# Weights of a fused attention and feed-forward kernel converted step by step, its mixing, gate and outputs regrouped

## The chip, the cores and the metric

The kernel runs as one program on one core of a Trainium2 chip. The metric is the device time of one execution in microseconds (us); the number quoted for a kernel is the median of its timed executions. A core has a matrix engine (PE in the profile, its weight loads shown apart as PEld), a vector engine (DVE), a scalar engine (ACT), GpSimd (POOL) and a queue engine (SP) that issues most of the transfers. DVE, ACT and POOL each work through their instructions in the order in which they were written; an instruction that waits holds up those behind it. Matrix products land in PSUM, which has eight banks.

## What is computed

Three stages follow each other, for a batch of 2 with 768 positions. The sizes are 8 heads of 64, a model width of 512, a mixing rank of 32, and feed-forward widths of 2048 and 1024. The inputs are float64.

```
mask   = argmax(q_n . c_n) == argmax(k_n . c_n)        # clustered attention, per head
x      = softmax(where(mask, q k^T / 8, -1e9)) v       # (2, 768, 512)

u      = x + ((x^T @ U) @ V)^T                         # mixing over the positions
x      = u + relu(u @ w_ch1) @ w_ch2                   # first feed-forward

h      = relu(x @ w_in)                                # second feed-forward, gated
conv   = conv_w[0]*h[s-1] + conv_w[1]*h[s] + conv_w[2]*h[s+1]
out    = (h * sigmoid(conv)) @ w_out
```

## The kernel before

**Three stages.** Attention runs over 96 steps (`step(n)`, 6 tiles for each of 16 heads). Then come the first feed-forward in 8 chunks of 256 columns and the second in 4. To keep float32 accuracy on the faster product format, every operand is split in a rounded high part and a low rest (`parts`: a cast on one engine, a subtraction on another), and each product is made of three: high by high, high by low, low by high.

**Code order is engine order.** Nothing is rescheduled. Work beside the products is placed by hand: generators yield after each group of matrix products, and `side(columns)` then issues one piece of waiting work: one entry of `aside`, one entry of `mixing`, and, for each 4096 columns of product, one `pump` of the weight conversion.

**Weights.** A chunk's weights come as float64 in jobs of 512 columns: two jobs for a wide matrix (`queue_wide`), two for a tall one (`queue_tall`). A job is a transfer (SP), a scaling (`job_base`, ACT), three integer operations on DVE (`job_word`: low, high, sign) that make a float32 word, and the put: a cast to the high part on ACT and a subtraction for the low part on POOL. The put of a wide matrix in the first feed-forward also forms four sums on POOL, and its last two casts on ACT (`rest`, L532) read those sums.

**First feed-forward.** `ff_h(c, b)` makes chunk c for batch element b by seven block products (Strassen's scheme) of 6 matrix products each, in four PSUM banks (`ps_a`); DVE combines them, ACT applies relu and casts (L822, L823) and POOL subtracts (L824). `ff_a(c, b)` makes eight groups `acc` of 6 products of 384 columns in three shared banks (`ps_t`, where mixing also lands); after each, DVE adds the bank to the sum `xa` (L845).

**Mixing** of one batch element is one entry `mt` (48 small products and the split of its result `tt`: per quarter a cast on ACT, a subtraction on DVE and a second cast on ACT), six entries `mu` (a product and a DVE addition of 128x512 onto x, L616), and six entries `mx` (four transposes and a copy on ACT). For the second batch element this stands after attention, between the groups of the first `ff_a(0, 0)` and `ff_h(1, 0)`; then `form_last` forms the operands of that element.

**Second feed-forward.** `g_h(c, b)` makes four groups `g` of 12 products; ACT applies relu into `h`. `gate(c, b)` makes, for two halves of 128x768 in SBUF, the convolution (one ACT instruction, two on DVE, L890 and L891), the sigmoid on ACT (L894), the product on POOL (L895), a cast on ACT and a subtraction on DVE (L900). `g_o(c, b)` makes six groups `po` of 6 products of 512 columns, each added to the output by DVE (L917, a copy on ACT for the first chunk).

## Time and profile before

| what | value |
|---|---|
| median of 3 executions | 715.45 us (715.01 to 715.98) |
| the profiled execution | 715.09 us, its span 713.3 us |
| busy share of the span | PE 92%, PEld 78%, DVE 71%, ACT 52%, POOL 41% |
| chain of work that ended last | PE 60%, DVE 22%, waiting to issue 7%, ACT 5%, POOL 5% |
| mean granted clock of PE | 0.98 of full speed |

The profile is one execution. A row of a stretch gives each engine's busy time and number of instructions, the clock that PE was granted (1.00 is full speed) and the load of the transfers. A row of time gives start, duration, engine, line, operation and tiles of an instruction, and in square brackets how long its engine had been idle before it and what it waited for. A row of waits gives who waited for whom: the sum in us, how often, and the longest. Ends of products on PE are modelled and overlap, so its pace is read from one start to another.

### The profile page before, as it was taken

To read this page: it belongs to the slowest core of one execution; us is meant where nothing else is said; L and a number is where in the kernel's file an instruction comes from. 1 tells how busy PE (TensorE), PEld (TensorE's weight loads), DVE (VectorE), ACT (ScalarE), POOL (GpSimd) and SP (SyncE) were. 2 spreads that over 40 slices of the span, in tenths; PEclk is the share of its full clock that TensorE was granted. 3 is DMA by queue.
4 is the path that set the end of the run, shared out by engine and by line. 5 is a ranking of instruction groups with operands and counts; after the bars stand their busy time and mean duration, and the time that the engine had idled before them with its cause. 6 is when DMAs were issued, how large, how long until landed. Compare 5 with 4: busy or idle time off the path is not lost.

```text
span 713.3 us, 10476 instructions
## 1 busy us (share of the span) xinstructions
PE 654.3 (92%) x3846; PEld 553.7 (78%) x3846; DVE 508.1 (71%) x890; ACT 371.9 (52%) x719; POOL 295.7 (41%) x299
## 2 busy tenths in 40 slices
PE   8999999999999987887799999999999698978896
PEld 5766767666767656887799999999989697966784
DVE  6887787878787656574657667584686768697665
ACT  6767667667676633443434344444443564653431
POOL 4645334535434624334635353636413432352221
PEclk9999999999999999999899999999999899999999
DMA  7687458354551011010212022130112110130003
GB/s 184 127 174 166 97 122 204 75 129 83 136 149 30 1 60 59 1 60 0 89 59 89 32 90 75 44 110 9 60 59 84 36 59 4 59 116 1 0 30 148
DMA packets 17860, 55.50 MB, mean 78 GB/s; under 512 B 3120, under 2 KB 3760, under 8 KB 17808
## 3 DMA queue, kind: packets, MB, share of 16 engines
q1 hardware_dynamic: 14208, 40.08, 18.5%
q0 software_dynamic: 3600, 14.75, 10.5%
q8 instruction: 30, 0.49, 0.3%
q14 instruction: 22, 0.18, 0.1%
HBM read 50.19 MB, written 3.15 MB: 75 GB/s over the span
## 4 chain that ended last, share of the span: by engine, by line
PE 60%; DVE 22%; issue 7%; ACT 5%; POOL 5%; DMA 0%; DVEq 0%; POOLq 0%
PE pv L399 8%; PE tr L383 7%; PE acc L841 4%; PE sc L345 4%; PE acc L842 3%; PE pb L781 3%; PE acc L843 3%; PE pd L781 3%; PE sc L356 3%; DVE cv L891 3%; PE pa L781 3%; PE g L876 3%; PE g L875 3%; PE g L874 3%; DVE e L362 3%
## 5 line engine op out<-in xcount | busy, mean ns | idle before, releaser
L841 PE MATMUL acc<-r,vh 128*128 128x384 f32 x256 | 90.1, 352 | 17.0 <-DVE xa L845 13.2
L362 DVE TENSOR_SCALAR_CACHE_REDUCE e<-sc 128x768 f32<-128x768 f32 x96 | 91.5, 954 | 12.2 <-PE sc L356 11.3
L374 ACT ACTIVATE e<-sc,nb 128x768 f32<-128x768 f32 x96 | 87.0, 906 | 9.5 <-DVE e L362 8.9
L842 PE MATMUL acc<-r,vh 128*128 128x384 f32 x256 | 88.0, 344 | 1.8 <-POOL r L824 1.8
L845 DVE TENSOR_TENSOR xa<-acc,xa 128x384 f32<-128x384 f32 x128 | 68.1, 552 | 29.4 <-PE acc L843 29.2
L843 PE MATMUL acc<-r,vl 128*128 128x384 f32 x256 | 87.8, 343 | 0.0
L383 PEld LDWEIGHTS tr<-identf,e 128*128 128x128 f32 x576 | 64.9, 140 | 25.7 <-issue 5.6
L383 PE MATMUL tr<-identf,e 128*128 128x128 f32 x576 | 81.2, 276 | 1.4 <-ACT tt L605 0.7
L399 PE MATMUL pv<-pt,rv 128*64 128x384 f32 x384 | 72.9, 498 | 0.0
L390 DVE COPY pt<-tr 128x384 f32<-128x384 f32 x96 | 53.0, 552 | 22.3 <-PE tr L383 21.4
L390 ACT COPY pt<-tr 128x384 f32<-128x384 f32 x96 | 46.1, 480 | 41.9 <-PE tr L383 41.8
L841 PEld LDWEIGHTS acc<-r,vh 128*128 128x128 f32 x256 | 49.6, 194 | 23.1 <-DVE xa L845 18.3
L547 POOL TENSOR_TENSOR vl<-wx,vh 128x512 fp32r<-128x512 f32 x24 | 32.9, 1371 | 72.0 <-ACT vh L546 67.6
L345 PE MATMUL sc<-ab 128*128 128x384 f32 x192 | 57.2, 380 | 2.0 <-ACT e L374 1.4
L895 POOL TENSOR_TENSOR h<-h,cv 128x768 f32<-128x768 f32 x16 | 32.1, 2007 | 53.0 <-ACT cv L894 51.8
L842 PEld LDWEIGHTS acc<-r,vh 128*128 128x128 f32 x256 | 49.8, 195 | 2.5 <-POOL r L824 2.3
L824 POOL TENSOR_TENSOR r<-q,r 128x384 fp32r<-128x384 f32 x16 | 16.2, 1014 | 81.1 <-ACT r L823 68.0
L843 PEld LDWEIGHTS acc<-r,vl 128*128 128x128 f32 x256 | 49.7, 194 | 0.0
L356 PE MATMUL sc<-cd 80*128 80x384 f32 x192 | 49.6, 340 | 0.0
L459 DVE SCALAR_TENSOR_TENSOR wy<-wb,wy 128x512 int32<-128x512 int32 (+1 forms) x44 | 30.1, 685 | 23.0 <-ACT wb L450 19.1
L399 PEld LDWEIGHTS pv<-pt,rv 128*64 128x64 f32 x384 | 24.3, 136 | 26.7 <-issue 24.4
L450 ACT ACTIVATE wb<-raw 128x512 f32<-128x512 f32 (+3 forms) x52 | 33.8, 649 | 10.3 <-DVE wx L463 6.7
(246 smaller groups left out, 1612.2 us busy)
## 6 DMA issues: line engine op xcount, KB each, us to landing
raw<-in_w_dram SPq DMA_DIRECT2D x32, 512.0 KB, 3.8
...
```

The lines of the kernel that those rows point to most:

```text
L345: nc.tensor.matmul(ps[:, f, 0:HS], ab[:, 0, c0:c0 + P], ab[:, 1, f * HS:(f + 1) * HS], start=True, stop=False)
L356: nc.tensor.matmul(ps[:, f, 0:HS], cd[0:80, 0, c0:c0 + P], cd[0:80, 1, f * HS:(f + 1) * HS], start=False, stop=True)
L362: nc.vector.tensor_scalar(out=e, in0=ps[:, :, 0:HS], scalar1=-SCALE, scalar2=3e38, op0=ALU.mult, op1=ALU.min, accum_out=nb,)
L374: nc.scalar.activation(e, ps[:, :, 0:HS], AF.Exp, scale=SCALE, bias=nb, accum_out=st["sum", n // NT][:, n % NT:n % NT + 1])
L383: nc.tensor.transpose(pt[:, k, :], e[:, i, k * P:(k + 1) * P], identf)
L390: (nc.scalar.copy if i == 0 else nc.vector.tensor_copy)(to, st.pop(("t", n, i)))
L399: nc.tensor.matmul(acc[i * D:(i + 1) * D], vts[b, h // 2][:, h % 2, k], pt[:, k, i * NK:(i + 1) * NK].rearrange("p a b -> p (a b)"), start ...
L781: nc.tensor.matmul(o, l[:, k, w], r[:, k], start=first and not more, stop=last, skip_group_check=more)
L841: nc.tensor.matmul(acc, wh[:, f, ds_], r[:, 0], start=f == 0, stop=False)
L842: nc.tensor.matmul(acc, wh[:, f, ds_], r[:, 1], start=False, stop=False)
L843: nc.tensor.matmul(acc, wl[:, f, ds_], r[:, 0], start=False, stop=f == 1)
L845: nc.vector.tensor_add(o, acc, o)
```

## The change

**Conversion.** `pump` with its plan for the feed-forward is replaced by `tick`. One tick issues at most one step of a put (`puts`) and at most one word step (`words`): the scaling, the first DVE operation, nothing, the second, the third. The put of a wide matrix is seven steps. Up to three finished words wait until the tile that they go to has been read for the last time (`opens`). Ticks come once for every 4, then 6, then 12 times 384 columns.

**Mixing.** The result is accumulated in PSUM: an entry `mx` is now three transposes of x and one product with `tt` into the same bank, followed by one copy on ACT; the six entries `mu` with their DVE additions are gone, and eight entries `mx` replace twelve. The second copy of `tt` is made by POOL. For the second batch element `mt` stands ahead of the first group of `ff_a(0, 0)`, and the last two groups of `ff_a(0, 0)` stand behind `ff_h(1, 0)`.

**Gate.** It works on quarters of 128x384 whose sums lie in the four banks of `ps_a`; the product moves from POOL to DVE, the last subtraction from DVE to POOL. It is issued in ten parts, three to four per group of products. The groups `g` land in `ps_t`.

**Outputs.** `g_o` takes two chunks at once: 12 products per group, one addition or copy where there were two. The order of the groups changes with it. The subtractions in `form_after` move from DVE to POOL.

The diff, cut:

```diff
+    def tick():
+        clock[0] += 1
+        for j in fly:
+            words.extend([lambda f=THIN[k], j=j: f(j) for k in sorted(THIN) if k > j["at"]])
+        fly.clear()
+        if puts and puts[0][0] in opened:
+            puts.pop(0)[1]()
+        if words:
+            words.pop(0)()
+        elif begun and clock[0] - begun[0]["at"] > 4 and len(full) < 3:
+            j = begun[0]
...
+            def last():
+                job_sign(j)
+                full.append(j)
+                x = j["x"].bitcast(F32)
+                steps = j["steps"](x) if "steps" in j else [lambda: j["put"](x)]
+                for i, f in enumerate(steps):
+                    puts.append((j["slot"], lambda f=f, i=i: (f(), full.pop(0) if i >= len(steps) - j["held"] else None)))
+            words.extend([low, lambda: None, lambda: job_high(j), last])
...
-            nc.gpsimd.tensor_sub(x2[:, :, 0], x2[:, :, 0], x1[:, :, 0])
-            wide[c] = (hi, lo)
...
+            def first():
+                wide[c] = [pool().tile([P, 2, 7, P], F32R, tag=f"w{k}", name=f"w{k}") for k in "hl"]
+                split(0, 1, x1[:, :, 0:1])
...
+                nc.scalar.copy(hi[:, :, o:o + n], v)
+                nc.gpsimd.tensor_sub(lo[:, :, o:o + n], v, hi[:, :, o:o + n])
+                whole.update((c, o + i) for i in range(n))
+            def sums():
+                nc.gpsimd.tensor_add(x2[:, :, 1], x1[:, :, 1], x2[:, :, 1])
+                nc.gpsimd.tensor_sub(x1[:, :, 1], x1[:, :, 0], x1[:, :, 1])
+            def more():
+                nc.gpsimd.tensor_sub(x1[:, :, 0], x2[:, :, 1], x1[:, :, 0])
+                nc.gpsimd.tensor_sub(x2[:, :, 0], x2[:, :, 0], x1[:, :, 0])
+            return [first, lambda: split(5, 2, x2), sums, more, lambda: None, lambda: split(1, 2, x1), lambda: split(3, 2, x2)]
...
         def evac(pt):
-            for c in range(ND):
-                src, cs = pt[c * R:(c + 1) * R], slice(c * P, (c + 1) * P)
+            by = [(pt[c * R:(c + 1) * R], slice(c * P, (c + 1) * P)) for c in range(ND)]
+            for src, cs in by:
                 nc.scalar.copy(tts[b][0:R, cs], src)
+            for src, cs in by:
...
-        def evac(pu):
-            nc.vector.tensor_add(X[b][:, t], X[b][:, t], pu)
-        return mm, evac
-    def mix_x(b, t):
-        def mm():
-            px = ps_t.tile([P, ND, P], F32, tag="t", name="mx")
-            for c in range(ND):
-                nc.tensor.transpose(px[:, c], X[b][:, t, c * P:(c + 1) * P], identf)
+            px = ps_t.tile([P, HS], F32, tag="t", name="mx")
...
         def evac(px):
...
             if i % 2:
-                form_round(b, ("B11", "B12", "B21", "B22")[i // 2])
+                form_round(b, ("B11", "B12", "B21", "B22")[i // 2], eng=nc.gpsimd)
...
+                o = ps_t.tile([P, HS], F32, tag="t", name="g")
...
     def gate(c, b):
...
+        def conv(f, t):
             w = cw[:, FPC * c + f]
-            nc.scalar.activation(cv[f], h[f], AF.Identity, scale=w[:, 1:2])
...
-        for f in range(2):
+            x = cv[f, t] = ps_a.tile([P, DM], F32, tag="abcd"[2 * f + t], name="cv")[:, 0:HS]
+            a, z = t * HS, (t + 1) * HS
+            nc.scalar.activation(x, h[f][:, a:z], AF.Identity, scale=w[:, 1:2])
+            for k, d in ((0, -1), (2, 1)):
+                lo, hi = max(a, -d), min(z, S - d)
+                o = x[:, lo - a:hi - a]
+                nc.vector.scalar_tensor_tensor(out=o, in0=h[f][:, lo + d:hi + d], scalar=w[:, k:k + 1], in1=o, op0=ALU.mult, op1=ALU.add)
+        def close(f, t):
+            x = cv.pop((f, t))
+            nc.scalar.activation(x, x, AF.Sigmoid)
+            o = h[f][:, t * HS:(t + 1) * HS]
+            nc.vector.tensor_mul(o, o, x)
+        def split(f):
             gh, gl = hs[c, b][f]
             nc.scalar.copy(gh, h[f])
-            nc.vector.tensor_sub(gl, h[f], gh)
+            nc.gpsimd.tensor_sub(gl, h[f], gh)
+        todo = [(conv, 0, 0), (conv, 0, 1), (conv, 1, 0), (close, 0, 0), (conv, 1, 1), (close, 0, 1), (close, 1, 0), (split, 0), (close, 1, 1), (split, 1)]
+        for part, *at in todo:
+            part(*at)
             yield
-    def g_o(c, b):
-        wh, wl = tall[NCH1 + c]
-        assert ("v", NCH1 + c) in whole, c
+    def g_o(cs, b):
+        assert all(("v", NCH1 + c) in whole for c in cs)
+        last = cs[-1] == NCH2 - 1
...
+            ts = slice(t * P, (t + 1) * P)
+            n = 0
+            for c in cs:
+                wh, wl = tall[NCH1 + c]
+                for f, (gh, gl) in enumerate(hs[c, b]):
+                    for g, w in ((gh, wh), (gh, wl), (gl, wh)):
+                        nc.tensor.matmul(po, g[:, ts], w[:, f], start=n == 0, stop=n == 6 * len(cs) - 1)
+                        n += 1
             o = xa[b].rearrange("p a s -> p (a s)")[:, t * DM:(t + 1) * DM]
...
                 nc.scalar.copy(o, po)
             else:
                 nc.vector.tensor_add(o, po, o)
...
+            lambda: None,
             lambda: form_diff(b, "T4", spot[3]),
-            lambda: form_round(b, "B22"),
             lambda: form_split(b, "T4"),
         ]
...
-    due = [0]
+    due = [0, 0, 2]
+    TICK, STEP = [4 * HS], [6 * HS]
...
     def side(columns):
         due[0] += columns
-        if aside:
-            aside.pop(0)()
-        if mixing:
+        begin()
+        due[1] += columns
+        while due[1] >= STEP[0]:
+            due[1] -= STEP[0]
+            if aside:
+                aside.pop(0)()
+        if due[2]:
+            due[2] -= 1
+        elif mixing:
             mm, evac = mixing.pop(0)
             evac(mm())
             if not mixing:
                 aside.extend(form_last(B - 1))
-        while due[0] >= 4 * DM * KW:
-            due[0] -= 4 * DM * KW
-            pump(FLOW)
+        while due[0] >= TICK[0]:
+            due[0] -= TICK[0]
+            tick()
...
     F = NCH1
     run(first)
-    pump(FLOW)
-    run(ff_a(0, 0))
+    mm, evac = mixing.pop(0)
+    evac(mm())
+    a = ff_a(0, 0)
+    run(a, 6)
     run(ff_h(1, 0))
-    queue_wide(2, to(2))
+    TICK[0] = 6 * HS
+    run(a)
     run(ff_a(1, 0))
...
     flush()
-    run(ff_h(1, 1))
+    opens("w2")
     run(ff_h(0, 1))
-    queue_wide(3, to(3))
+    opens("w3")
...
+    opens(f"v{F}")
     spare_tiles += [x for b in range(2) for k in ("T2", "T3", "T4") for x in tok[b][k]]
-    run(g_h(0, 0), 12 * HS)
-    later(gate(0, 0))
+    run(g_h(0, 0), columns=12 * HS)
     run(ff_a(F - 1, 1, form_after(1)))
-    queue_tall(F + 1, to(F + 1))
...
+    STEP[0] = 4 * HS
+    aside.extend([lambda g=gate(0, 0): next(g, None)] * 10)
+    opens(f"v{F + 1}")
+    TICK[0] = 12 * HS
+    run_g(1, 0)
+    run_g(0, 1)
+    opens(f"w{F + 2}")
+    spare_tiles += [ring[1].tile([P, KW, HS], F32R, tag="r", name="g4") for _ in range(4)]
+    run_g(1, 1)
+    opens(f"w{F + 3}")
+    run_o((0, 1), 0)
+    run_g(2, 0)
+    run_o((0, 1), 1)
+    opens(f"v{F + 2}", f"v{F + 3}")
+    run_g(3, 0)
+    run_g(2, 1)
+    run_g(3, 1)
+    run_o((2, 3), 0)
+    run_o((2, 3), 1)
```

What moves on the engines stands below at three places, rows of before first, those of after second. A row is one instruction, or several alike in a row (x4): line, operation, result tile, sources and shape.

DVE, around the mixing of the second batch element at the start of `ff_a(0, 0)` (`acc` onto `xa` is the addition of a group, `tt1` the low part of the split, `mu` an addition of mixing, `wy` and `wx` word steps):

```order
L845 TENSOR_TENSOR xa_2608<-acc_3233,xa_2608 128x384
L604 TENSOR_TENSOR tt1_281<-mt_3241,tt1_281 32x128 x4
L845 TENSOR_TENSOR xa_2608<-acc_3278,xa_2608 128x384
L616 TENSOR_TENSOR x_2086<-x_2086,mu_3286 128x512
L456 TENSOR_SCALAR wy_3294<-raw_3165 128x512
L459 SCALAR_TENSOR_TENSOR wy_3294<-wb_3231,wy_3294 128x512
L463 SCALAR_TENSOR_TENSOR wx_3293<-wb_3231,wy_3294 128x512
L845 TENSOR_TENSOR xa_2608<-acc_3298,xa_2608 128x384
L616 TENSOR_TENSOR x_2086<-x_2086,mu_3306 128x512
L845 TENSOR_TENSOR xa_2608<-acc_3309,xa_2608 128x384
```

```order
L848 TENSOR_TENSOR u_3088<-pd_3137,u_3088 128x384
L647 TENSOR_TENSOR tt1_281<-mt_3210,tt1_281 32x128 x4
L882 TENSOR_TENSOR xa_1990<-acc_3244,xa_1990 128x384
L467 SCALAR_TENSOR_TENSOR wx_3252<-wb_3079,wx_3098 128x512
L882 TENSOR_TENSOR xa_1990<-acc_3254,xa_1990 128x384
L458 TENSOR_SCALAR wy_3270<-raw_2981 128x512
L882 TENSOR_TENSOR xa_1990<-acc_3272,xa_1990 128x384
```

The four subtractions of `tt1` now stand ahead of the first addition of `ff_a(0, 0)`, the additions of `mu` are gone, and the three word steps no longer stand in a row.

ACT, from the first cast of the wide weights of chunk 3 (`wh`, from the words `wx`) to the last one; `r`, `u`, `v` and `q` are relus and casts of the seven block products of `ff_h`, `wb` is a scaling:

```order
L518 CAST wh_3885<-wx_3823 128x2x128
L519 CAST wh_3885<-wx_3859 128x2x256
L822 ACTIVATE v_3830<-v_3830 128x384
L823 CAST r_3905<-v_3830 128x384
L822 ACTIVATE u_3829<-u_3829 128x384
L823 CAST r_3916<-u_3829 128x384
L532 CAST wh_3885<-wx_3823 128x2x256
L532 CAST wh_3885<-wx_3859 128x2x256
L450 ACTIVATE wb_3924<-raw_3849 128x512
```

```order
L562 CAST wh_3848<-wx_3782 128x2x128
L450 ACTIVATE wb_3852<-raw_3751 128x512
L859 ACTIVATE q_3818<-q_3818 128x384
L860 CAST r_3862<-q_3818 128x384
L562 CAST wh_3848<-wx_3838 128x2x256
L863 ACTIVATE r_3878<-pa_3821 128x384
L859 ACTIVATE v_3820<-v_3820 128x384
L860 CAST r_3891<-v_3820 128x384
L859 ACTIVATE u_3819<-u_3819 128x384
L860 CAST r_3905<-u_3819 128x384
L562 CAST wh_3848<-wx_3782 128x2x256
L450 ACTIVATE wb_3921<-raw_3808 128x512
```

The casts of one put (L518, L519 and two of L532 before, four of L562 after) lie in seven rows before and stand over eleven after, with relus between the last two.

DVE, where the first gate stands, `cv` being its convolution and sigmoid (`u` is `form_after`'s subtraction):

```order
L845 TENSOR_TENSOR xa<-acc,xa 128x384
L890 SCALAR_TENSOR_TENSOR cv<-h,cw,cv 128x767
L891 SCALAR_TENSOR_TENSOR cv<-h,cw,cv 128x767
L845 TENSOR_TENSOR xa<-acc,xa 128x384
L746 TENSOR_TENSOR u_3467<-xa,u_3466 128x768
L890 SCALAR_TENSOR_TENSOR cv<-h,cw,cv 128x767
L891 SCALAR_TENSOR_TENSOR cv<-h,cw,cv 128x767
L845 TENSOR_TENSOR xa<-acc,xa 128x384 x2
L746 TENSOR_TENSOR u_3463<-xa,u_3462 128x768
L456 TENSOR_SCALAR wy<-raw 128x512
L459 SCALAR_TENSOR_TENSOR wy<-wb,wy 128x512
L463 SCALAR_TENSOR_TENSOR wx<-wb,wy 128x512
```

```order
L882 TENSOR_TENSOR xa<-acc,xa 128x384 x4
L933 SCALAR_TENSOR_TENSOR cv<-h,cw,cv 128x383
L933 SCALAR_TENSOR_TENSOR cv<-h,cw,cv 128x384 x2
L933 SCALAR_TENSOR_TENSOR cv<-h,cw,cv 128x383 x2
L933 SCALAR_TENSOR_TENSOR cv<-h,cw,cv 128x384
L939 TENSOR_TENSOR h<-h,cv 128x384
L933 SCALAR_TENSOR_TENSOR cv<-h,cw,cv 128x384
L933 SCALAR_TENSOR_TENSOR cv<-h,cw,cv 128x383
L939 TENSOR_TENSOR h<-h,cv 128x384
L458 TENSOR_SCALAR wy<-raw 128x512
L939 TENSOR_TENSOR h<-h,cv 128x384 x2
L461 SCALAR_TENSOR_TENSOR wy<-wb,wy 128x512
```

The instructions on halves of 128x767 became ones on quarters, products `h` by `cv` joined them, and the subtractions `u` went to another engine.

## Rows read from the trace of the kernel before

**Rows 1.** The page's busy time, share of the span and instructions of each engine.
```profile
PE 654.3 (92%) x3846; PEld 553.7 (78%) x3846; DVE 508.1 (71%) x890; ACT 371.9 (52%) x719; POOL 295.7 (41%) x299
```

**Rows 2.** Stretches: length, busy (xcount) PE, PEld, DVE, ACT, POOL, clock, DMA share, GB/s.
```profile
258.00:304.00 46.00, 36.06 (x231) 31.77 (x229) 29.46 (x52) 20.04 (x42) 18.06 (x16) 0.96 0.14 47
304.00:360.00 56.00, 45.60 (x224) 43.91 (x223) 34.08 (x58) 22.07 (x43) 28.02 (x28) 0.88 0.17 57
360.00:540.00 180.00, 174.88 (x993) 171.27 (x992) 123.44 (x221) 74.25 (x142) 78.48 (x78) 1.00 0.18 59
540.00:566.00 26.00, 19.56 (x98) 18.10 (x97) 19.15 (x26) 12.13 (x18) 8.11 (x5) 0.87 0.25 81
566.00:709.20 143.20, 128.09 (x625) 112.60 (x623) 102.25 (x113) 67.39 (x106) 43.95 (x25) 0.99 0.14 48
```

**Rows 3.** Timeline of PE (start, duration, ...), 48 products of 384 columns apart.
```profile
383.75 0.33 PE L841 MATMUL acc<-r,vh 128*128 128x384 f32 x1
...
392.07 0.33 PE L781 MATMUL pa<-u,wh 128*128 128x384 f32 x1
```

**Rows 4.** Timeline of PE, 36 products of 512 columns apart.
```profile
574.31 0.39 PE L910 MATMUL po<-vh,u 128*128 128x512 f32 x1
...
582.51 0.33 PE L874 MATMUL g<-u,wh 128*128 128x384 f32 x1
```

**Rows 5.** Waits from 258 to 713 us: who for whom, sum, times, longest.
```profile
ACT cv L894 <- DVE cv L891: 30.0, 13, 3.2
...
ACT wh L532 <- POOL wx L525: 18.5, 6, 4.3
...
PE po L910 <- DVE xa L917: 13.6, 7, 2.4
...
PE acc L841 <- DVE xa L845: 13.2, 9, 4.0
...
PE pb L781 <- DVE u L793: 7.2, 3, 3.9
```

**Rows 6.** Timeline at the mixing of the second batch element.
```profile
262.96 0.45 PE L841 MATMUL acc<-r,vh 128*128 128x384 f32 x1 [2.64 <-ACT r L823]
...
265.86 2.33 PE L596 MATMUL mt<-x,uw 128*32 128x128 f32 x48
...
271.81 0.50 PE L612 MATMUL mu<-tt,v 96*128 96x512 f32 x1 [2.37 <-ACT tt L605]
```

**Rows 7.** Timeline at the put of the wide weights of chunk 3.
```profile
322.69 0.62 ACT L532 CAST wh<-wx 128x512 fp32r<-128x512 f32 x1 [3.31 <-POOL wx L525]
...
324.44 0.56 DVE L793 TENSOR_TENSOR u<-pb,q 128x384 f32<-128x384 f32 x1 [7.95 <-POOL r L824]
...
325.06 0.62 PE L781 MATMUL pb<-u,wh 128*128 128x384 f32 x2 [3.94 <-DVE u L793]
```

**Rows 8.** Timeline at three word steps in a row.
```profile
352.41 0.70 DVE L459 SCALAR_TENSOR_TENSOR wy<-wb,wy 128x512 int32<-128x512 int32 x1 [4.02 <-ACT wb L450]
...
353.75 1.48 DVE L845 TENSOR_TENSOR xa<-acc,xa 128x384 f32<-128x384 f32 x3
...
354.35 0.69 PE L841 MATMUL acc<-r,vh 128*128 128x384 f32 x1 [4.04 <-DVE xa L845]
```

**Rows 9.** Timeline of a gate, DVE and POOL.
```profile
578.41 1.02 DVE L891 SCALAR_TENSOR_TENSOR cv<-h,cw,cv 128x767 f32<-128x767 f32 x1
...
581.07 2.03 POOL L895 TENSOR_TENSOR h<-h,cv 128x768 f32<-128x768 f32 x1 [0.49 <-ACT cv L894]
...
581.43 2.48 DVE L891 SCALAR_TENSOR_TENSOR cv<-h,cw,cv 128x767 f32<-128x767 f32 x1
```

**Rows 10.** Groups over the span: line, engine, tiles, xcount | busy, mean ns | idle before.
```profile
L624 PE MATMUL mx<-identf,x 128*128 128x128 f32 x48 | 7.3, 275 | 1.3 <-DVE xa L845 1.3
...
L746 POOL TENSOR_TENSOR u<-xa,u 128x768 fp32r<-128x768 f32 x4 | 7.4, 1847 | 5.5 <-ACT u L745 5.3
...
L917 DVE TENSOR_TENSOR xa<-po,xa 128x512 f32<-128x512 f32 x36 | 23.9, 682 | 19.8 <-PE po L912 19.8
```

More of the change, by code (lines that the diff above doesn't have):

```diff
@@ L494, in pump, with begin, low @@
             j = jobs.pop(0)
-            j["at"], j["plan"] = 0, plan
+            j["at"] = 0
             job_dma(j)
             fly.append(j)
+    words, puts = [], []
+    clock = [0]
+    begun, opened, full = [], set(), []
+    def begin():
+        while jobs and len(begun) < 2:
+            j = jobs.pop(0)
+            job_dma(j)
+            j["at"] = clock[0]
+            begun.append(j)
+    def tick():
[9 more added lines that the diff above has]
+            j = begun[0]
+            job_base(j)
+            def low():
+                job_low(j)
+                begun.pop(0)
+                begin()
+            def last():
+                job_sign(j)
+                full.append(j)
+                x = j["x"].bitcast(F32)
+                steps = j["steps"](x) if "steps" in j else [lambda: j["put"](x)]
+                for i, f in enumerate(steps):
+                    puts.append((j["slot"], lambda f=f, i=i: (f(), full.pop(0) if i >= len(steps) - j["held"] else None)))
+            words.extend([low, lambda: None, lambda: job_high(j), last])
@@ L542, in put_whole @@
+        jobs.append({"slot": ("w", c), "held": 2, "src": [(0, flat[:, UN:2 * UN])], "steps": steps})
     def put_whole(to, shape, tag, c, pool, o, x):
@@ L990, in tile_kernel @@
     ring.append(rb)
+    opened.update({("w", 1), ("v", 1)})
     def pool_of(c):
@@ L1038, in flush, with run, run_g, run_o @@
             aside.pop(0)()
-    def run(gen, columns=6 * HS):
-        for _ in gen:
+    def run(gen, n=99, columns=6 * HS):
+        while n and next(gen, True) is None:
             side(columns)
-    def later(gen):
-        aside.extend([lambda: next(gen, None)] * 7)
+            n -= 1
+    def run_g(c, b):
+        run(g_h(c, b), columns=12 * HS)
+        aside.extend([lambda g=gate(c, b): next(g, None)] * 10)
+    def run_o(cs, b):
+        run(g_o(cs, b), columns=12 * DM)
+    def queue(*what):
+        for k in what:
+            (queue_wide if k[0] == "w" else queue_tall)(int(k[1:]), to(int(k[1:])))
+    def opens(*what):
+        opened.update((k[0], int(k[1:])) for k in what)
     F = NCH1
     run(first)
-    pump(FLOW)
-    run(ff_a(0, 0))
+    mm, evac = mixing.pop(0)
+    evac(mm())
+    a = ff_a(0, 0)
+    run(a, 6)
     run(ff_h(1, 0))
-    queue_wide(2, to(2))
+    TICK[0] = 6 * HS
+    run(a)
     run(ff_a(1, 0))
+    queue("w2", "w3", "v2", "v3", "w4", "v4")
+    jobs.append(conv_job)
+    for c in range(5, F):
+        queue(f"w{c}", f"v{c}")
+    queue(*(f"{k}{F + c + i}" for c in range(0, NCH2, 2) for k in "wv" for i in range(2)))
+    run(ff_h(1, 1))
     flush()
-    run(ff_h(1, 1))
+    opens("w2")
     run(ff_h(0, 1))
-    queue_wide(3, to(3))
+    opens("w3")
     run(ff_a(1, 1))
-    queue_tall(2, to(2))
+    opens("v2")
     run(ff_h(2, 0))
     run(ff_a(0, 1))
-    queue_tall(3, to(3))
+    opens("v3")
     run(ff_h(2, 1))
-    queue_wide(4, to(4))
+    opens("w4")
     run(ff_a(2, 0))
```

160 lines of the change are left out of this document (57 added, 103 removed).

## The prediction, on record before the changed kernel ran

> **What bounds the kernel now.** I read the page's busy shares first, then the stretches, then PE's own timeline for its pace, then who waits for whom, and last the timelines of the longest waits.
>
> PE has 92% busy, the next engine 71% [rows 1], so the end is set by PE's work plus the time in which PE gets none. The change alters hardly any product (it adds 16 of 384 columns for 12 `mu` of 512). So the question is how much PE loses behind attention and how much of that stays.
>
> PE's pace where nothing holds it: from one `acc` to a `pa` 48 products later 392.07 - 383.75 = 8.32 us, 0.1733 each [rows 3]; 36 products of 512 columns in 582.51 - 574.31 = 8.20 us, 0.228 each [rows 4]. By that `ff_h` (42 products) takes 7.28 us, `ff_a` and `g_h` (48) 8.32, `g_o` of one chunk (36) 8.20. I lay this on the five stretches [rows 2]:
>
> - 258 to 304: 231 products, of which 138 belong to `ff_a(0,0)`, `ff_h(1,0)`, `ff_a(1,0)` and 15 to the end of attention: 153 x 0.1733 = 26.5; `mt` 2.33 [rows 6]; six `mu` 1.4; 24 transposes between a third of 0.1733 and 7.3/48 = 0.152 each [rows 10], 1.4 to 3.6. Sum 31.6 to 33.8 of 46: lost 12.2 to 14.4.
> - 304 to 360: three `ff_h` and two `ff_a`, 222 x 0.1733 = 38.5 of 56: lost 17.5.
> - 360 to 540: eleven of each, 171.6 of 180: lost 8.4.
> - 540 to 566: `g_h(0,0)` and the last `ff_a`, 16.6 of 26: lost 9.4.
> - 566 to 709.2: seven `g_h`, eight `g_o`, 58.2 + 65.6 = 123.8 of 143.2: lost 19.4.
>
> Together 67 to 69 us. The two stretches that lose the largest part have mean clocks of 0.88 and 0.87, between PE's levels of 1.2 and 2.4 GHz, the others 0.96 to 1.00 [rows 2]; PE's idle 3.94 and 4.04 us [rows 7, 8] both fall in the stretch with 0.88. What the clock takes is inside the lost time, and I let it go with the waits.
>
> The profiled execution took 715.1, 0.4 below the median of 715.45, so the sum on it stands for the median within a measurement. With no loss behind 258 us the time would be 715.1 - 67 to 69 = 646 to 648; I take 647.
>
> **Part by part: what stays.**
>
> Conversion by ticks. Before, a put of wide weights runs at one place: POOL forms sums, ACT's cast of `wx` stands 3.31 us waiting for them, POOL's `r` comes late, DVE's addition waits 7.95 us and PE 3.94 [rows 7]. That ACT wait sums to 18.5 us over 6 puts [rows 5]. After, the casts stand over eleven instructions of ACT, relus between the last two, so the first relu no longer stands behind both sums. POOL's work is the same; it comes as seven steps of at most two subtractions or sums, some 1 us each (half of the 1.85 of a subtraction of 768 [rows 10]), one step per group of 6 x 0.1733 = 1.04 us. The word steps: three DVE instructions in a row, the second of which waited 4.02 us for ACT's `wb`; behind them three additions of `xa` stood ready, and PE waited 4.04 [rows 8]. After, one of them, 0.70 us, stands between two additions of 1.48/3 = 0.49 each: 1.19 per group of 1.04, but only in three ticks of five, so DVE keeps up; three banks cover it. The added waits: ACT's cast waits for POOL's sums still (up to two sums); behind it stands a relu, for which `r` and POOL wait. I cost a steady chunk at nothing if the three banks cover it; over the chunks 3 to 7 together 1 us (0 to 3, the top being one sum of 1 us in three of them). Chunk 2, whose weights are opened one stage before their use: its last casts end shortly before `ff_h(2,0)`: 1 us (0 to 3).
>
> Mixing. The six `mu` and their additions of DVE go (0.68 each, by the like additions of L917 [rows 10]: 6 x 0.68 = 4.1 us for this element). The first `mu` waited 2.37 us for `tt` [rows 6], ACT's cast standing between two DVE subtractions; after, the four casts stand together ahead of the first group, and two groups pass before the first `mx`. New: `mt` now stands ahead of PE's `acc` of `ff_a(0,0)`, which had waited 2.64 us for `r` [rows 6], so its 2.33 us lie in that wait. It costs 1.5 (0 to 3): below, `r` is early; above, the four subtractions hold the last DVE steps of `ff_h(0,0)`. Then the forming of the second element's operands: nine DVE subtractions of about 1 us (the 1.02 of two operands in SBUF [rows 9]) in the time of about 12 groups (12.5 us), beside 12 additions of 0.5: 15.2 of 12.5, the excess of 2.7 partly in three banks: 1 us (0 to 2.7).
>
> Gate. Before, DVE needs 4 x 1.02 plus two subtractions of like length, undisturbed, but one convolution step took 2.48 us where POOL's product ran from 581.07 to 583.10 [rows 9]. ACT's sigmoid waited 30.0 us in 13 places for it [rows 5]. After, twelve quarters: eight convolution steps and four products; by the three additions with a PSUM operand in 1.48 [rows 8] 0.49 each, 5.9 us. Word steps add at most 2.1 (three of 0.70). So DVE has 8.0 us of work per `g_h` of 8.32: close, and ACT is near that as well. The subtractions go to POOL, 2 x 1.85 [rows 10], off DVE. A wait is new: `g` shares three banks of `ps_t`, and ACT's relu, which frees one, stands behind sigmoids that wait for DVE; who waits is PE's next `g`. Two parts lie between a convolution and its sigmoid, about 1.4 us, for two DVE steps of 1.0. I take 2 us for eight gates (0 to 6, two bank waits of 0.7 in half of them).
>
> The Trainium skill has a rule against these quarters: in "Perfetto Trace Analysis", section "Optimizing Scalar/DVE Operations", a DVE instruction pays some 125 ns of its own on PSUM and some 60 on SBUF, so larger instructions help an engine that is saturated. An estimate by that page: 12 x 0.125 - 6 x 0.06 = 1.1 us more per gate, 9 over eight, which would make 662. The rows here speak for less: three PSUM additions of half the length come in 1.48, a long step in SBUF takes 1.02, so two quarters cost 0.98.
>
> Outputs. 24 additions of `po` go: 24 x 0.68 = 16.4 us of DVE [rows 10], and with them what holds PE there: 13.6 us in 7 waits of up to 2.4 [rows 5]. A bank is now wanted every 12 x 0.228 = 2.7 us. Nothing stays.
>
> `form_after` on POOL: 1.85 for about 1 on DVE, at four places per element, off DVE; POOL is 31% busy in the last stretch [rows 2]. Its result is needed some groups later: nothing, or a single 1.85 within the range. Attention: the first element's mixing is spared its DVE additions too, below 1 us of gain; I take 0.7.
>
> Sum: 647 + 1 + 1 + 1.5 + 1 + 2 - 0.7 = 652.8, say **653**. All residues at their tops: 647 + 3 + 3 + 3 + 2.7 + 6 + 1.85 = 667.
>
> **Rivals.**
>
> (1) POOL and ACT stay the wait at the puts. POOL takes more subtractions, and every cast still waits for the sums. For it: POOL is already 50% busy in 304 to 360 (28.0 of 56 [rows 2]). Against: the steps lie apart. Price: seven wide puts, each between the 8.4/5 = 1.7 us that a put cost at most in the quiet stretch and the 3.94 of [rows 7]: 12 to 28; with the other residues 664 to 680, middle 670.
>
> (2) Quarters in PSUM are slowed by POOL like the halves, factor 2.48/1.02 = 2.4 [rows 9]. With POOL busy 45 to 60% of a gate's time (two subtractions of 1.85, some steps of a put) 5.9 x (1 + 0.6 x 1.4) + 2.1 = 13 per 8.32: up to 4.6 x 8 = 37, of which `g_o`, with few additions, takes back about half: 660 to 685, middle 670. Against: additions with a PSUM operand took 0.49 and 0.56 [rows 7, 8], none near the double. The page "SBUF — State Buffer", section "Who interferes with whom", of the Trainium skill says that only a DVE instruction with two SBUF inputs contends with GpSimd's reads; [rows 9] agrees for two SBUF inputs, and no row shown here tests the other case.
>
> (3) Slower than before: the gate's parts run one behind the other, each waiting on another engine's in-order queue. A quarter's convolution is 0.62 on ACT (by the cast in [rows 7]) and two of 0.49 on DVE, its close 0.62 and 0.49, a split one and a half of that cast, 0.93, and 1.85: 4 x 1.6 + 4 x 1.1 + 2 x 2.8 = 16.4 us, where the ten parts have 3.3 groups of 2.08, 6.9. Excess 9.5 x 8 = 76, in place of the 2 above: 727. It ends above 715 once the excess per gate passes (715 - 651)/8 = 8 us. For it: the 30.0 us of sigmoids [rows 5]. Against: the order puts two other parts between dependent ones.
>
> (4) The waits merely move, and nothing changes: 715. The order of instructions shows the word steps and casts apart and the additions gone, so this is unlikely.
>
> **How the numbers follow.** Forecast 653 (647 to 663): 0.65. Rival 1: 0.22; 2: 0.07; 3: 0.05; 4: 0.01. The range 647 to 675 holds nearly all of the first, three quarters of 1 and half of 2: 0.64 + 0.16 + 0.04 = 0.84. Faster, by over 0.2% (1.4 us, about what a measurement of this kernel can tell): 0.94; same 0.01; slower 0.05.
>
> **What would show it.** Right: in the profile after, five to seven us between the pace and the length over all behind attention; clock 0.97 or more in each of the five stretches; no PE wait over 2 us at a put; no waits of `po` for additions; DVE quarters at about 0.5 to 0.55. Rival 1 would show ACT's `wh` behind POOL's `wx`, PE behind `u`; rival 2 quarters of over 0.8 beside POOL; rival 3 PE's `g` behind ACT's `h`. The largest doubts are the gates, where DVE and ACT are both near 8 us of 8.3, and chunk 2, whose weights come at the last moment; each could add 5 us that I have not.

## The result and the profile after

The changed kernel takes 652.91 us (652.71 to 653.23), against 715.72 for the kernel before in the same comparison: a ratio of 0.911 (0.908 to 0.914). Forecast were 653.0 and 647 to 675. The profiled execution took 652.71 us, 62.4 less than the profiled one of before.

The page's busy shares, to be read against [rows 1]:

```profile
PE 636.4 (98%) x3850; PEld 545.8 (84%) x3850; DVE 459.0 (71%) x894; ACT 372.3 (57%) x747; POOL 307.5 (47%) x309
```

PE went from 92 to 98%. DVE has 49 us less to do, 10% of its work, at the same share of a span that is 9% shorter. The stretches, columns as in [rows 2]; the bounds lie at the same products, but the first stretch begins one block product earlier, at the `pa` that stood at 256.37 us before:

```profile
252.85:291.53 38.68, 36.05 (x241) 32.26 (x240) 27.32 (x44) 20.48 (x41) 21.06 (x19) 1.00 0.10 28
291.53:331.64 40.11, 39.31 (x224) 38.35 (x223) 28.76 (x54) 20.74 (x41) 23.45 (x25) 1.00 0.24 76
331.64:503.24 171.60, 171.60 (x992) 171.60 (x991) 123.49 (x232) 77.17 (x149) 91.10 (x87) 1.00 0.24 75
503.24:519.88 16.64, 16.64 (x98) 16.64 (x97) 9.55 (x17) 6.62 (x11) 6.59 (x5) 1.00 0.30 95
519.88:646.75 126.87, 124.91 (x624) 111.86 (x624) 74.28 (x129) 72.43 (x139) 45.68 (x28) 1.00 0.13 44
```

The clock is 1.00 in all five; 0.88 and 0.87 are gone [rows 2]. In the third and fourth PE is busy all the time, and 171.60 and 16.64 are what its pace of 0.1733 us per product gives. The stages, each from the product at which it begins to that of the next, in us:

| stage | before | after | gain | forecast |
|---|---|---|---|---|
| to the last `pa` of `ff_h(0,0)` | 256.37 | 252.85 | 3.5 | 0.7 |
| `ff_a(0,0)`, mixing, `ff_h(1,0)`, `ff_a(1,0)` | 47.8 | 38.7 | 9.1 | 9.7 to 11.9 |
| `ff_h(1,1)` to `ff_a(0,1)` | 55.9 | 40.1 | 15.8 | 16.5 |
| eleven `ff_h` and `ff_a` | 179.9 | 171.6 | 8.3 | 7.4 |
| first `g_h`, last `ff_a` | 26.0 | 16.6 | 9.4 | 9.4 |
| second feed-forward | 143.6 | 127.3 | 16.3 | 17.4 |

Whom PE still waits for behind attention, to be read against [rows 5]:

```profile
PE acc L879 <- POOL r L861: 1.3, 2, 0.9
PE acc L878 <- DVE xa L882: 1.1, 2, 0.5
PE pb L818 <- POOL wl L563: 0.8, 1, 0.8
PE po L962 <- ACT h L913: 0.8, 1, 0.8
```

The 13.6 us of `po` for `xa`, and nearly all of the 13.2 of `acc` for `xa`, are gone. ACT's casts still wait 18.7 us in 7 places for POOL's sums, as long as before; the put of chunk 3 shows how that can cost nothing now (timeline):

```profile
327.74 0.62 ACT L562 CAST wh<-wx 128x512 fp32r<-128x512 f32 x1 [1.54 <-POOL wx L572]
...
331.64 0.51 PE L818 MATMUL pa<-u,wh 128*128 128x384 f32 x2
```

The cast stands in an `ff_a` here, and PE begins the `ff_h` behind it without a wait. Before, the put fell into an `ff_h`, and PE stood 3.94 us [rows 7].

### The profile page after: what moved, and what is told of

It is laid out like the page before. It is cut to its first block, busy times and chain, and to the rows that moved or that the text cites. A ratio compares the mean times of both kernels' runs of the same rounds, so it can differ in the third digit from the quotient of the medians.

```text
span 650.9 us, 10539 instructions
## 1 busy us (share of the span) xinstructions
PE 636.4 (98%) x3850; PEld 545.8 (84%) x3850; DVE 459.0 (71%) x894; ACT 372.3 (57%) x747; POOL 307.5 (47%) x309
## 4 chain that ended last, share of the span: by engine, by line
PE 44%; DVE 3%; ACT 3%; POOL 2%; issue 1%; POOLq 0%; DVEq 0%; ACTq 0%
PE po L962 8%; PE acc L879 6%; PE acc L878 6%; PE acc L880 6%; PE pd L818 4%; PE pb L818 4%; PE pa L818 4%; PE g L910 2%; PE g L911 2%; PE g L912 2%; DVE cv L933 2%; PE pc L818 2%; DVE h L939 1%; POOL wl L563 0%; ACT cv L929 0%
## 5 line engine op out<-in xcount | busy, mean ns | idle before, releaser
L878 PE MATMUL acc<-r,vh 128*128 128x384 f32 x256 | 86.7, 339 | 1.3 <-DVE xa L882 1.1
L879 PE MATMUL acc<-r,vh 128*128 128x384 f32 x256 | 85.8, 335 | 1.3 <-POOL r L861 1.3
L882 DVE TENSOR_TENSOR xa<-acc,xa 128x384 f32<-128x384 f32 x128 | 69.7, 553 | 22.9 <-PE acc L880 22.8
L880 PE MATMUL acc<-r,vl 128*128 128x384 f32 x256 | 85.6, 335 | 0.0
L589 POOL TENSOR_TENSOR vl<-wx,vh 128x512 fp32r<-128x512 f32 x24 | 30.8, 1294 | 64.7 <-ACT vh L588 64.7
L933 DVE SCALAR_TENSOR_TENSOR cv<-h,cw,cv 128x383 f32<-128x383 f32 (+1 forms) x64 | 38.2, 621 | 26.1 <-ACT cv L929 24.9
L878 PEld LDWEIGHTS acc<-r,vh 128*128 128x128 f32 x256 | 48.0, 188 | 4.1 <-DVE xa L882 3.6
L879 PEld LDWEIGHTS acc<-r,vh 128*128 128x128 f32 x256 | 48.1, 188 | 1.9 <-POOL r L861 1.9
L880 PEld LDWEIGHTS acc<-r,vl 128*128 128x128 f32 x256 | 48.0, 188 | 0.0
L399 PEld LDWEIGHTS pv<-pt,rv 128*64 128x64 f32 x384 | 24.6, 136 | 26.8 <-issue 24.5
L563 POOL TENSOR_TENSOR wl<-wx,wh 128x512 fp32r<-128x512 f32 (+1 forms) x32 | 36.5, 1156 | 11.9 <-ACT wh L562 11.5
```

The source lines that it names most:

```text
L399: nc.tensor.matmul(acc[i * D:(i + 1) * D], vts[b, h // 2][:, h % 2, k], pt[:, k, i * NK:(i + 1) * NK].rearrange("p a b -> p (a b)"), start ...
L878: nc.tensor.matmul(acc, wh[:, f, ds_], r[:, 0], start=f == 0, stop=False)
L879: nc.tensor.matmul(acc, wh[:, f, ds_], r[:, 1], start=False, stop=False)
L880: nc.tensor.matmul(acc, wl[:, f, ds_], r[:, 0], start=False, stop=f == 1)
L882: nc.vector.tensor_add(o, acc, o)
```

## The experiments

The theory: the sum of the prediction, by which each part takes away a wait of its own and, with the others in place, is worth what its rows show. Its rivals stand in the expectations. Each kernel is the changed one with one part undone, or a place in it altered; its median is compared with 652.9, its stages with those above. The kernel before took 715.7 to 720.2 us in these comparisons, so a difference of a few us is read from the stages of the profiled executions: the eleven `ff_h` and `ff_a` take 171.6 us again in e3_out, e4_sbuf, e5_engines, e6_mix, i5_three, f1_late, f2_form and h1_gate, whose edits leave them alone.

**e1_words: a job's three word steps in a row.**

```diff
-            words.extend([low, lambda: None, lambda: job_high(j), last])
+            words.extend([lambda: None, lambda: (low(), job_high(j), last()), lambda: None, lambda: None])
```

> The three word steps of a job stand in a row again (one tick issues all three, two ticks after the scaling, so that DVE need not wait for ACT); all else is as after the change. Theory, spacing matters: a burst of 3 x 0.68 = 2.0 us and two additions behind it exceed what three banks of 1.04 us cover now and then; part of the 8.4 us lost from 360 to 540 before comes back, 3 to 8 us: 656 to 661. Rival, before it was the wait of DVE for wb ahead of the burst (4.02 us) that cost, not the burst: the three banks cover 2.0 us and the time is 652.9 within 1.

670.87 us, ratio to before 0.934 (0.931 to 0.937): 18 slower, more than either expected. Nearly every `ff_a` takes 0.3 to 2.4 us more. From the one that lost most (timeline):

```profile
329.29 0.68 DVE L458 TENSOR_SCALAR wy<-raw 128x512 int32<-128x512 int32 x1
...
331.06 0.66 ACT L450 ACTIVATE wb<-raw 128x512 f32<-128x512 f32 x1
...
331.75 0.70 DVE L461 SCALAR_TENSOR_TENSOR wy<-wb,wy 128x512 int32<-128x512 int32 x1 [1.79 <-ACT wb L450]
...
333.76 0.45 PE L878 MATMUL acc<-r,vh 128*128 128x384 f32 x1 [1.85 <-DVE xa L882]
```

The scaling was issued two ticks earlier and still came late: ACT had three casts of puts of 0.6 us each ahead of it, among those of `ff_h`, and DVE, having begun the burst, could not turn to its additions. Here the rival's wait and the theory's burst are one mechanism: the burst is dear because its middle waits for an engine that is itself behind.

**e2_put: the seven steps of a put in one tick.**

```diff
-                for i, f in enumerate(steps):
-                    puts.append((j["slot"], lambda f=f, i=i: (f(), full.pop(0) if i >= len(steps) - j["held"] else None)))
+                if steps:
+                    puts.append((j["slot"], lambda: ([f() for f in steps], [full.pop(0) for _ in range(j["held"])])))
```

> The seven steps of a wide put are issued in one tick again; all else is as after the change. Theory, the spread steps are what keeps POOL and ACT from holding ff_h: some 7.6 us of POOL work in a row come back before r, with ACT's casts waiting for the sums, and PE waits 1.2 to 3.9 us at each of six or seven puts: 660 to 680. Rival, in the new order the put falls into ff_a, where POOL has no r to make, and the spreading is worth nothing: 653 to 655.

680.51 us, 0.947 (0.944 to 0.951): 28 slower, at the top of the theory's range. The kernel before issued a put in two pieces, one `pump` apart, so this is denser than before, and not only the change undone. Three `ff_a` take 14.2 in place of 8.3 to 8.6. The chain is not the one that I named (timeline):

```profile
320.54 0.62 ACT L562 CAST wh<-wx 128x512 fp32r<-128x512 f32 x1 [4.72 <-POOL wx L572]
...
322.57 0.70 DVE L461 SCALAR_TENSOR_TENSOR wy<-wb,wy 128x512 int32<-128x512 int32 x1 [5.69 <-ACT wb L450]
...
323.78 0.69 PE L878 MATMUL acc<-r,vh 128*128 128x384 f32 x1 [4.37 <-DVE xa L882]
```

POOL's sums hold ACT's cast, the cast holds the scaling `wb` behind it, that holds a word step on DVE, and that holds the addition which frees PE's bank: four engines, each in order.

**e3_out: a group for each chunk's outputs.**

```diff
-        run(g_o(cs, b), columns=12 * DM)
+        for c in cs:
+            run(g_o((c,), b), columns=6 * DM)
```

> Each chunk's output is a group of its own again (6 products, one addition or copy each; 24 more evacuations, of which 12 additions on DVE for chunk 1 in place of nothing and 12 for chunk 3); the order of the groups stays. Theory, as predicted: the additions themselves held PE before (13.6 us in 7 waits of po for xa) and some of it comes back: 657 to 667. Rival: those waits came from DVE being held by the gate's long steps (2.48 us beside POOL), which are gone; a bank is wanted every 1.37 us and DVE has little else there: 653 to 655.

665.78 us, 0.927 (0.924 to 0.930). The three output stretches take 23.1, 18.2 and 38.3 us, where they took 18.7, 16.4 and 32.9: 11.7 more. (The profiled execution also lost 1.7 us ahead of its second group of scores.) The rival's time fails: even with short gate steps, PE stands behind additions (timeline):

```profile
628.49 2.46 DVE L933 SCALAR_TENSOR_TENSOR cv<-h,cw,cv 128x383 f32<-128x383 f32 x4 [0.78 <-ACT cv L929]
...
631.59 0.50 PE L962 MATMUL po<-vh,u 128*128 128x512 f32 x1 [1.60 <-DVE xa L968]
```

Four convolution steps stand ahead of an addition for a bank that is wanted every 1.37 us. But the rival's mechanism is half right. PE's waits for additions are 3.3 us in 4; 4.7 us in 3 are for ACT's relus, which free the same banks, and the granted clock of the first output stretch is 0.85, where it was 1.00. In the kernel before, each of the seven waits of `po` for `xa` stands right behind a convolution step of 1.92 to 2.47 us, beside POOL (timeline of before):

```profile
596.68 2.47 DVE L891 SCALAR_TENSOR_TENSOR cv<-h,cw,cv 128x767 f32<-128x767 f32 x1
...
599.07 1.27 DVE L917 TENSOR_TENSOR xa<-po,xa 128x512 f32<-128x512 f32 x2
...
599.80 0.50 PE L910 MATMUL po<-vh,u0T4h 128*128 128x512 f32 x1 [1.94 <-DVE xa L917]
```

So those 13.6 us belong to the gate and the outputs together.

**e4_sbuf and e5_engines: the gate's quarters in SBUF, and then the engines of before too.** The four quarters lie in `ff_h`'s three temporaries, idle by then, and one tile more.

```diff
-            x = cv[f, t] = ps_a.tile([P, DM], F32, tag="abcd"[2 * f + t], name="cv")[:, 0:HS]
+            k = "quvc"[2 * f + t]
+            x = cv[f, t] = tmp.get(k, cvp).tile([P, HS], F32, tag=k, name="cv")
```

> The gate's quarters lie in SBUF tiles in place of PSUM banks; parts, engines and order are as after the change. Theory, PSUM is what frees DVE from POOL: with two operands in SBUF the steps beside POOL's subtractions take 1.2 to 1.5 us for a quarter, the mean of L933's line goes from 0.62 to 0.75 or more, and 64 + 32 such steps cost DVE 10 us or more; PE loses 2 to 8: 655 to 661. Rival, quartering and spreading is what counts: alone in SBUF a quarter takes about 0.5, the mean stays at 0.6, and the time is 652 to 654.

e5_engines changes two lines more:

```diff
-            nc.vector.tensor_mul(o, o, x)
+            nc.gpsimd.tensor_mul(o, o, x)
-            nc.gpsimd.tensor_sub(gl, h[f], gh)
+            nc.vector.tensor_sub(gl, h[f], gh)
```

> As e4_sbuf (the gate's quarters in SBUF), and the engines as before the change too: the product on POOL, the last subtraction on DVE. Theory, contention for SBUF between DVE and POOL is the cost and PSUM the cure: POOL's work per gate grows from two subtractions to four products, so more of DVE's steps meet it: slower than e4_sbuf by 2 to 8 us, 672 to 678. Rival, the product on DVE (0.89 us each in e4_sbuf) was the cost in e4_sbuf: without it DVE has fewer steps and the time falls below e4_sbuf's 669.9, to 660 to 668.

669.90 us, 0.935 (0.930 to 0.940), and 672.56, 0.938 (0.936 to 0.940). The gate's groups, of the changed kernel, then of e4_sbuf (groups by shape from 519 us on):

```profile
L933 DVE SCALAR_TENSOR_TENSOR cv<-h,cw,cv 128x383 f32<-128x383 f32 x32 | 19.1, 621 | 25.5 <-ACT cv L929 24.9
...
L939 DVE TENSOR_TENSOR h<-h,cv 128x384 f32<-128x384 f32 x32 | 17.1, 550 | 6.3 <-ACT cv L937 6.3
```

```profile
L940 DVE TENSOR_TENSOR h<-h,cv 128x384 f32<-128x384 f32 x32 | 28.1, 892 | 6.0 <-ACT cv L938 6.0
L934 DVE SCALAR_TENSOR_TENSOR cv<-h,cw,cv 128x383 f32<-128x383 f32 x32 | 25.3, 810 | 24.8 <-ACT cv L930 24.2
```

Same sizes, same order; with the second operand in SBUF a product takes 0.89 us on average in place of 0.55, and the steps of 128x383 take 0.81 in place of 0.62. DVE pays some 19 us more, and the kernel takes 17 more. The mean hides two cases (timeline of e4_sbuf):

```profile
631.77 1.82 POOL L945 TENSOR_TENSOR u1x<-h,u1x 128x768 fp32r<-128x768 f32 x1 [6.56 <-ACT u1x L944]
632.09 1.92 DVE L940 TENSOR_TENSOR h<-h,cv 128x384 f32<-128x384 f32 x1 [0.85 <-ACT cv L938]
...
640.22 0.55 DVE L940 TENSOR_TENSOR h<-h,cv 128x384 f32<-128x384 f32 x1
```

With POOL idle, the 20 products and 48 steps in SBUF take 0.55 and 0.61 us, as in PSUM; the 10 products and 12 steps that lie mostly beside a POOL instruction take 1.65 and 1.29 on average. In PSUM POOL does not show: 15 steps beside it take 0.62, like the 39 with POOL idle. So it is POOL, and not SBUF as such, that costs, and PSUM, not the quartering, carries the gate's part: the theory holds, and its price of 2 to 8 us was far too low. e5_engines is 2.7 slower than e4_sbuf, the side that the theory named, but the executions of the two overlap (669.1 to 674.8 and 671.6 to 673.7); in the profiled ones the second feed-forward takes 146.4 and 143.4. The rival, 660 to 668, falls. POOL's quarter products take 1.38 us on average there.

**e6_mix: mixing as before, for both elements.** The old `mu`, `mx` and split (L596 to L630 of the kernel before), no group skipped, the forming ended ahead of `ff_h(1,1)`.

> Mixing as before the change (products mu and an addition on DVE each, then the transposes; the split with its casts and subtractions in turn; one entry per group from the first group of ff_a(0,0)); the rest as after. Theory: the 12 additions of 0.68 and the waits for tt come back; attention ends some 3 us later and the stretch up to ff_h(1,1) takes 4 to 8 us more: 659 to 665. Rival, the spread word steps alone had freed DVE there: 653 to 656.

665.57 us (662.88 to 668.28), 0.928 (0.925 to 0.932). In the trace the first `ff_h` begins at 247.5 in place of 243.0 us, and from the end of `ff_h(0,0)` to the end of `ff_h(0,1)` it takes 55.4 in place of 49.7; the first `mu` of the second element waits 2.4 us for `tt` again, as in [rows 6]. The attention's second part, of before and of the changed kernel (stretches; DVE's busy time is the third):

```profile
150.00:256.37 106.37, 102.80 (x673) 71.28 (x672) 80.48 (x163) 70.86 (x152) 49.23 (x48) 1.00 0.32 76
```

```profile
150.00:252.85 102.85, 102.29 (x673) 71.76 (x673) 78.88 (x162) 70.61 (x151) 50.57 (x49) 1.00 0.36 89
```

All of attention's gain lies behind 150 us, where the first element is mixed, and it goes when mixing is undone. It is PE's idle time: 3.6 us before, 0.6 after. This kernel takes back the additions, the products and the split at once, and what each of them costs was not run apart.

**e7_form: `form_after` subtracts on DVE.**

```diff
-                form_round(b, ("B11", "B12", "B21", "B22")[i // 2], eng=nc.gpsimd)
+                form_round(b, ("B11", "B12", "B21", "B22")[i // 2])
```

> The eight subtractions of form_after on DVE again; the rest as after. Theory: DVE has room in these ff_a (0.55 of each 1.04 us, word steps spread), so 0.95 per second group costs up to 2 us: 653 to 655. Rival: these subtractions were what held DVE in the stretch that lost 9.4 us: 658 to 662.

661.05 us, 0.922 (0.920 to 0.924): 8 slower, the rival's time. DVE has room, but not in order (timeline):

```profile
523.53 0.96 DVE L782 TENSOR_TENSOR u<-xa,u 128x768 fp32r<-128x768 f32 x1 [0.90 <-ACT u L781]
524.41 0.68 DVE L467 SCALAR_TENSOR_TENSOR wx<-wb,wy 128x512 int32<-128x512 int32 x1
525.00 1.02 DVE L882 TENSOR_TENSOR xa<-acc,xa 128x384 f32<-128x384 f32 x2
...
525.61 0.44 PE L878 MATMUL acc<-r,vh 128*128 128x384 f32 x1 [1.61 <-DVE xa L882]
```

Seven of the eight subtractions cost DVE 0.96 and 0.90 of waiting for the cast just issued on ACT, the first 1.38 and 1.33; with a word step, 0.68, that is 2.54 us ahead of an addition.

**Can the rest be had?** What the changed kernel still loses: 5.7 us around mixing and forming, 1.6 up to `ff_a(0,1)`, 3.5 (127.3 - 123.8) in the second feed-forward. Four kernels try to get some of it.

i5_three: `mixing` twice per group in `ff_h(1,0)`; `TICK[0] = 4 * HS` from `opens("w2")` to the end of `ff_a(1,1)`; the copies of chunk 0's outputs on DVE.

> Three places where the changed kernel still loses time, each in its own stretch: two entries mx per group in ff_h(1,0), so that forming the second element's operands starts two groups earlier; ticks every 4 x 384 columns from the opening of w2 to the end of ff_a(1,1); the copies of chunk 0's outputs on DVE in place of ACT. Theory: forming loses 4.3 us, because DVE needs 0.55 + 0.95 per 1.04 us group, and two more groups give back 1 to 2; ff_h(2,0) gives back 1; the output stretch 1 to 2: 648.5 to 650.5. Rival: DVE is full there, the work only moves, 652 to 654.

662.29 us, 0.923 (0.921 to 0.926), slower than either expected: the first edit costs 3.6 us in its stage, the second 5.3, the third changes nothing (0.2 less). With denser steps the chain of e2_put is back (timeline):

```profile
320.39 0.62 ACT L562 CAST wh<-wx 128x512 fp32r<-128x512 f32 x1 [4.17 <-POOL wx L572]
...
321.60 0.70 DVE L461 SCALAR_TENSOR_TENSOR wy<-wb,wy 128x512 int32<-128x512 int32 x1 [3.37 <-ACT wb L450]
...
323.64 0.69 PE L878 MATMUL acc<-r,vh 128*128 128x384 f32 x1 [3.43 <-DVE xa L882]
```

f1_late: `due = [0, 0, 4]`, and `run_o((0, 1), 0)` ahead of `run_g(1, 1)`.

> Two edits in separate stretches: mixing of the second element starts two groups later, so that forming its operands moves out of ff_h(1,0), the other way than in i5_three; and the outputs of chunks 0 and 1 of the first element stand ahead of g_h(1,1), so that at first two g_h and not three follow each other. Theory for the first: forming in ff_h(1,0) puts DVE's and POOL's long instructions (2.49 and 1.71 us beside each other) ahead of r, so later is better: the 60 groups of acc take 12.5 to 14 in place of 14.7. Rival: it is DVE's sum that counts (9 x 0.95 in ten groups): 15 to 17. For the second: DVE and ACT have 9 us of work per g_h of 8.32 where words come too; with two in a row the 3.3 us lost in g and the first po fall to 0.5 to 2. Together 649.5 to 652.5.

661.86 us, 0.920 (0.917 to 0.923), slower than expected. From the first `acc` to the end of `ff_h(0,1)` it takes 48.6 in place of 48.1: the loss moves from the 60 products of `acc` (13.1 from 14.7) into the `ff_h` around them. The outputs, put earlier, catch up with the gate that they need (timeline):

```profile
541.35 0.50 PE L962 MATMUL po<-vh,u0T4h 128*128 128x512 f32 x1 [2.70 <-ACT u0T4h L943]
...
543.25 0.50 PE L962 MATMUL po<-vh,u0T4l 128*128 128x512 f32 x1 [1.17 <-POOL u0T4l L944]
```

The first output stretch takes 24.5 in place of 18.7, the second 19.4 in place of 16.4. The third `g_h` in a row was cover for a gate.

f2_form: forming's two POOL subtractions on DVE.

> The two subtractions that forming the second element's operands has on POOL go to DVE; all else as after. Theory, contention: the differences on DVE that took 2.49 and 1.28 us beside POOL's 1.85 fall to 0.95, POOL's r is no longer late, which is worth as much as the two more steps of 0.95 cost: the 60 products of acc take 14 to 15 us as now, 652 to 653.5, and no DVE step there takes over 1.0. Rival, only DVE's sum of work counts: 15.5 to 17, 654 to 655.

653.23 us, 0.908 (0.905 to 0.911): the same time. DVE's 2.49 falls to 0.95, as the theory has it (one step still takes 1.75 beside POOL's `r`), and the two steps more take it back: the 60 products of `acc` take 14.9 in place of 14.7.

h1_gate: a gate begins with two convolutions and a close; the weights from chunk 2 on are queued ahead of `ff_a(1,0)`.

> Two edits in separate stretches. The parts of a gate start with two convolutions and a close in place of three convolutions, so that DVE gets four steps and one product and not six steps (3.65 us) in the first group of 2.08 us; and the weights of chunk 2 are queued eight groups earlier, so that their words are ready when w2 opens. Theory for the gate: what PE loses in the first three g_h and the po behind them (3.3 us) comes from that front load: 0.5 to 1.5 left. Rival: ACT's sigmoid waits 1.2 us for DVE at once, the relu of g behind it: 4 to 8 lost. For the words: the 1.3 us lost in ff_h(2,0) goes, but up to six word steps of 0.68 come into the forming stretch, which loses 1 to 4 more. Together 650 to 655.

651.19 us (651.08 to 651.90), 0.908 (0.902 to 0.913): 1.7 below the changed kernel, the fastest of the study. The ratios' intervals overlap, the executions of the two kernels do not. From 519 us on it gains 2.2 us, the first output stretch 16.75 in place of 18.65. The front load on DVE was the cause there: 3.65 us of steps in a row in the changed kernel, 2.46 now (DVE at the third gate, of the changed kernel, then of h1_gate):

```profile
543.66 3.65 DVE L933 SCALAR_TENSOR_TENSOR cv<-h,cw,cv 128x383 f32<-128x383 f32 x6 [1.39 <-ACT cv L929]
```

```profile
544.18 2.46 DVE L933 SCALAR_TENSOR_TENSOR cv<-h,cw,cv 128x383 f32<-128x383 f32 x4 [1.16 <-ACT cv L929]
...
545.50 0.47 ACT L937 ACTIVATE cv<-cv 128x384 f32<-128x384 f32 x1 [0.84 <-DVE cv L933]
```

The rival's wait is there too, 0.84 us, but PE's one wait for a relu there is 0.2 us, in place of 0.8 and 0.3. Queueing earlier frees `ff_h(2,0)` of its 1.35 and costs the two `ff_h` ahead 1.5.

## Why the prediction was right, step by step

**The frame held.** PE's pace and its lost time by stretch say where the time came from, and the change left little of that loss. That the sum met the median to 0.1 us is luck, because its errors cancel. Behind attention 5.7 + 1.6 + 3.5 = 10.8 us are left where the sum has 6.5, so the sign of "five to seven us" did not come; attention gave 2.8 more than the sum takes, and the base of 647 was some 1.5 us too high. Of the other signs, the clock, the puts and the outputs came as named; of the gate's quarters, named at 0.5 to 0.55, the products did with 0.55 and the steps, 0.62, did not.

**Attention was mis-sized**: 3.5 us gained, 0.7 taken. I took below 1 us without a row for it. In the kernel before, PE's waits of over 0.25 us behind 150 us are six, 3.4 us together, between 152 and 203 us, while the six additions `mu` lie between 155 and 203; the waits come back with mixing as before (e6_mix).

**Mixing and forming were mis-sized the other way**: 2.5 us forecast, 5.7 left. The prediction had 15.2 us of DVE work in 12.5 us and let three banks swallow most of the excess. It forgot that DVE's step with two operands in SBUF slows beside POOL's subtraction, and that POOL's `r` comes late too:

```profile
276.61 1.85 POOL L782 TENSOR_TENSOR u<-xa,u 128x768 fp32r<-128x768 f32 x1 [0.48 <-ACT u L781]
276.78 2.49 DVE L793 TENSOR_TENSOR spot<-xa 128x768 f32<-128x768 f32 x1
...
280.17 0.44 PE L879 MATMUL acc<-r,vh 128*128 128x384 f32 x1 [0.94 <-POOL r L861]
```

f2_form shows that this alone is not the loss: with those subtractions on DVE the sum of DVE's work is as long, and so is the time.

**Puts and words** were right in sign and place: the steady stages lose nothing, below the 1 us that I kept; for chunk 2 the 1 us (0 to 3) became 1.35. Rival 1 did not come; e2_put, with its puts denser than in either kernel, shows its mechanism and ends at 680, the top of its range.

**Gate**: 2 us forecast, with the outputs 3.5 lost. A quarter's step takes 0.62 and a product 0.55, not 0.49, which was the pace of three additions in a row and not the length of one: 8 x 0.62 + 4 x 0.55 = 7.2 us per gate, not 5.9. Four steps of 1.02 and two of 0.95, the lengths of halves in SBUF with POOL idle, are 6.0, so by this estimate the quarters cost 1.2 us more per gate than halves would. That is near the estimate of 1.1 that I made by the Trainium skill's "Perfetto Trace Analysis", section "Optimizing Scalar/DVE Operations". Its higher price for PSUM does not show, though: quarters in SBUF take as long with POOL idle, 0.61 and 0.55 (e4_sbuf), so what is paid here goes with the number of instructions, wherever the operand lies. And PE lost 3.5 us in that whole stage, not 9 by this alone.

Rival 2 did not come: no quarter in PSUM shows POOL. e4_sbuf is that rival's case without PSUM, at 670, the middle that I gave it. The Trainium skill's rule in "SBUF — State Buffer", section "Who interferes with whom", agrees here: the additions, steps and products of DVE with one SBUF input take the same time beside POOL as without it, and with two a product goes from 0.55 to 1.65. (The page also has DVE contend in its two-port modes, which the prediction's "only" leaves out.) The kernel before could have settled this rival: its additions of `acc`, with one operand in PSUM, take 0.55 us both in the 43 cases with POOL idle and in the 67 that lie mostly beside a POOL instruction. Rival 3 did not come; ACT's wait for DVE in the gate fell from 30.0 us [rows 5] to 3.2.

**Outputs** came as forecast, with no wait of `po` for additions left, but the reason was half right: before, what held DVE was the convolution step ahead of each addition, so the gate's change took part in these 13.6 us. With that change in place, separate groups still cost 11.7 (e3_out). **`form_after`** I put at nothing left, and nothing is: both its `ff_a` run at PE's pace. The subtractions are worth more than the 0.95 of DVE that I counted for each, as a wait on ACT goes with it: undone they cost 8 (e7_form).

Undone one at a time, words, puts, outputs, gate, mixing and `form_after` cost 18.0 + 27.6 + 12.9 + 19.6 + 12.7 + 8.1 = 99 us, where 62.8 were gained together. So these costs are not shares of the gain. The put in one tick is worse than the form of before, and gate and outputs share the same waits; I think that the parts also cover each other, with one engine's delay holding the next, but that is not shown. Which part would gain what alone on the kernel before was not run.
